# One store of twelve score tiles, a cubic for the exponentials of one attention and one product for both: gated pair of attentions on one core

## The chip, the core and the metric

The kernel runs on one core of a Trainium2 chip. The metric is the device time of one execution in microseconds; the median of three executions before the change is 1826.78 us (1826.64 to 1827.12).

## The reference

Two attentions, A and B, read the same x (2048 tokens of 512 values, 32 heads of 16). A has one key and one value head for all its query heads, B has its own for each. A gate per token mixes them.

```python
def _A_ref(x, wq, wk, wv, wo):
    ...
    scores = jnp.einsum("bhqd,bkd->bhqk", q, k) * (Dh ** -0.5)
    p = _softmax(scores, axis=-1)
    o = jnp.einsum("bhqk,bkd->bhqd", p, v)
    return (lambda x, *d: x.transpose(*d))(o, 0, 2, 1, 3).reshape(B, S, H * Dh) @ wo
...
g = _sigmoid((x * gate_w).sum(-1, keepdims=True))
a = _A_ref(x, A_wq, A_wk, A_wv, A_wo)
b = _B_ref(x, B_wqkv, B_wo)
return g * a + (1 - g) * b
```

All of it is float32. The weights A_wq and A_wk are drawn eight times larger than the others, so the scores of A are large and those of B small.

## The kernel before

**The work.** The heads of each attention go in four groups of eight, in the order A0, B0, A1, B1 and so on. A group goes through four phases (two halves of 1024 queries, each with two sets of four heads); there are 32 phases. A phase has 32 quads, two for each block of 128 keys; a quad is two score tiles of 128 x 1024, so there are 2048 score tiles. For each, TensorE makes the scores (`products`, eight matmuls of 64x32 with 512 columns in float16, into one of two PSUM banks `sc`), then the exponential goes to SBUF. When both tiles of a quad are there, its V product (`values`, float32) adds to a PSUM accumulator `pair[0]`; the ones among the columns of V give the softmax denominators in the same product.

**Two ways to an exponential.** Most tiles go through ScalarE (`score`, one ACTIVATE of 128 x 1024). The others go through VectorE (`chain`): the scores land in the spare bank `pair[1]`, and seven VectorE instructions make the exponential: a conversion to an integer, two bit operations that part exponent and mantissa, and four multiply-adds (`horner`). ScalarE writes into six tiles `prob`, VectorE works in six tiles `vec`.

**Beside it** run the projections of the next group (24 jobs of eight matmuls for each half of q, k and v, `project`), their layout by DMA, and for each finished half of a group the output products (`o_unit`): for each of four pairs of token blocks six jobs of eight matmuls into the spare bank, VectorE multiplies by the gate into one of two tiles `sums`, and a DMA adds that to the output in HBM. Ahead of it `normalised` brings the accumulator's rows in place by DMA, takes reciprocals of 128 x 512 denominators and multiplies. The last output, that of group B3, is added on chip to what HBM held (`late`), and written.

**The order** of each engine's instructions is written out by a planner in the kernel (`_Plan`, `pe_step`, `spare_job`, `value_job`), which goes by costs (`EXP`, `HALF`, `PRODUCT`) and due times. The next score stands at the earliest where a bank comes free; other work may stand ahead of it as long as it starts at most SLACK = 404 ns after the start of the ACTIVATE before it. For the second score of a quad this lateness holds only for V products of VectorE's quads (the lines with `LATE`). A V product stands whole (512 columns) where 860 ns are left up to the next score, else as two halves of 256.

Of the kernel before, what the change touches and what calls it, by code (L numbers as in the profile page):

```python
# [20 lines left out]
P = 128  # L21
# [6 lines left out]
NG = 4  # L28
# [7 lines left out]
S_MAX = 40.0  # L36


VEC = (0.14718679, 0.3602188, 0.76941108, -0.03925424)
LEAD = struct.unpack("I", struct.pack("f", 3.46474126))[0] & 0x7FFFFF  # L40
# [3 lines left out]
EXP, EXP_ENDS, EXP_AFTER = 904, 1136, 456  # L44
# [6 lines left out]
PROBS, VECS = 6, 6  # L51
# [116 lines left out]
def _fast(ctx, tc, x, wq_a, wk_a, wv_a, wo_a, wqkv_b, wo_b, gate_w, out, flag):  # L168
# [23 lines left out]
    sums = [big.tile([P, 2, BLK], F32, name=f"sum{n}") for n in range(2)]  # L192
# [82 lines left out]
    x_tiles = (vec_tiles + sums)[:8]  # L275
# [145 lines left out]

    def project(part, src, gi, half, kind, can, due):
# [17 lines left out]
        def finish(t):  # L440
# [9 lines left out]
            def then(end):  # L450
                free["spare"] = end + FROM_VEC
                plan.vec(lambda: absmax(kind, 2 * gi + half, hilo[0], AX.XY), 1130, 4, end, due=end + 8000)
                if part == "v":
                    turned(gi, half, hilo, end)
                else:
                    put(hilo, end)
# [6 lines left out]
                     lambda now: ready.get(need, math.inf) <= now and free["hilo"] <= now and can(), due, name, lambda now: can())  # L463

    def turned(gi, half, hilo, now):
# [26 lines left out]
        units.append(_Unit(jobs, finish, lambda now: True, lambda: 0, f"turn{gi}{half}"))  # L492
# [3 lines left out]
    def o_unit(n, half, t, qs, first, last):  # L496

        src, gi = groups[n]
        w, i = weights[src, gi, "o"], "ab".index(src)
        steps = [(q, a, b) for q in qs for a, b in PARTS]  # L500
        tt = [8 * half + t, 8 * half + 4 + t]
        mine = late[:, 4 * half + t]
        state = {}

        def job(k):
            q, a, b = steps[k]
            lhs = [o16s[n, half, q][:, a, t * P : (t + 1) * P]] * 2
            rhs = [w[e ^ (q // 2)][:, b] for e in range(2)]
            by_tiles(pair[1], lhs, rhs, k == 0, k == len(steps) - 1)

        def finish(end):
            def take(e):
                g = gate_up[:, i, tt[e] : tt[e] + 1]
                if n + 1 == len(groups):
                    nc.vector.scalar_tensor_tensor(mine[:, e], pair[1][:, e], g, mine[:, e], op0=ALU.mult, op1=ALU.add)  # L515
                    if last:
                        (nc.sync, nc.scalar)[e].dma_start(out[tt[e] * P : (tt[e] + 1) * P, :], mine[:, e])
                    return
                if e == 0:
                    state["sum"] = sums[state["turn"]]  # L520
                nc.vector.tensor_scalar(state["sum"][:, e], pair[1][:, e], g, None, op0=ALU.mult)  # L521

            def then(t):
                free["spare"] = t + FROM_VEC
                if n + 1 == len(groups):
                    return
                dst = out.rearrange("(h e t p) d -> h t p e d", h=2, e=2, p=P)[half, t_]
                if n == 0:
                    done = plan.on_sp([lambda: nc.sync.dma_start(dst, state["sum"])], t, ISSUE_SP)
                else:  # L530
                    done = plan.on_pool([lambda: nc.gpsimd.dma_start(dst, state["sum"], accum_op=ALU.add)], t, 1300)  # L531
                sum_free[state["turn"]] = done + SUM_LANDS

            t_ = t
            begin = end + TO_VEC
            if n + 1 < len(groups):
                state["turn"] = turn[0]
                turn[0] ^= 1
# [6 lines left out]
        due = 32 * (4 * n + 2 * half + 8)  # L545
        return _Unit(jobs, finish, lambda now: all(made(("o16", n, half, q), math.inf) <= now for q in qs)
                     and made(("wo", src, gi), math.inf) <= now and made("gates", math.inf) <= now
                     and (sum_free[turn[0]] <= now + 4000 if n + 1 < len(groups) else made("late", math.inf) <= now), lambda: starts_in(due), f"o{n}{half}{t}")

    turn, sum_free = [0], [0.0, 0.0]  # L550

    def normalised(n, half, q, raw, now):
# [10 lines left out]
        moves = [(*move, e) for t in (d, o) for e in range(2) for move in moves if move[0] is t]  # L563
        for m, (part, at, to, n_rows, e) in enumerate(moves):
            queues[m % len(queues)].dma_start(part[ROWS * e + to :][:n_rows], raw[at, e])
        plan.sp = max(plan.sp, now) + len(moves) * ISSUE_SP
        o16 = ops.tile([P, 2, BLK], F16, tag="o16", name=f"o16{n}{half}{q}", bufs=7)
# [5 lines left out]

        def times(c):
            nc.vector.scalar_tensor_tensor(o[:, c : c + cut], o[:, c : c + cut], UP, d[:, c : c + cut], op0=ALU.mult, op1=ALU.mult)
# [10 lines left out]
        due = now + 30000  # L586

# [3 lines left out]
        for c in range(0, BLK, cut):  # L591
            a = plan.vec(lambda c=c: over(c), 1560, 3.5, now + 7700, (), None, due)
            b = plan.vec(lambda c=c: times(c), 330, 3.4, now + 12000, (a,), None, due)
            e = plan.vec(lambda c=c: high(c), 200, 3.3, 0.0, (b,), None, due)
# [873 lines left out]
```

## Time and profile before

| what | value |
|---|---|
| median of three executions | 1826.78 us |
| span of the profiled execution | 1822.2 us |
| so outside the span, against the median | 4.6 us |
| ScalarE busy | 1778.7 us, 98% |
| TensorE busy | 1742.1 us, 96% |
| VectorE busy | 1332.0 us, 73% |
| score tiles on ScalarE / on VectorE | 1926 / 122 |

The profile gives one time for the profiled execution, its span, from the first to the last instruction. "Busy" of an engine is the time in which at least one of its instructions was under way; a matmul's end is modelled, so TensorE's share says little on how much room it has. A group of rows names its source line, the engine, what was written from what, the shapes, the count, the busy time and the mean time of one. A float32 product appears as two matmuls per matmul of the source. "issue" as a releaser means that nothing in the profile explains the wait.

### The profile page before, as it was taken

What the parts mean: (1) busy time and instruction counts of PE and PEld (TensorE: products, weight loads), DVE (VectorE), ACT (ScalarE), POOL (GpSimd) and SP (SyncE); (2) the same over time, 40 slices, a digit from 0 to 9 for tenths busy, and PEclk for the clock granted to TensorE, in tenths of its full rate; (3) what the DMA queues carried; (4) which work ended last, traced back from release to release, by engine and by line L of the source; (5) the groups of instructions that cost most, each with busy time, mean ns of one, the idle gap of its engine ahead of it and who ended that gap; (6) DMA issues with size and microseconds to landing.
All of it is one profiled execution on the core that took longest, in us unless ns stands there. A gap on an engine that the chain in (4) does not pass through costs nothing.

```text
span 1822.2 us, 95700 instructions
## 1 busy us (share of the span) xinstructions
PE 1742.1 (96%) x44697; PEld 844.5 (46%) x44697; DVE 1332.0 (73%) x1507; ACT 1778.7 (98%) x1942; POOL 305.1 (17%) x367
## 2 busy tenths in 40 slices
PE   8999999999999999999999999999999999999896
PEld 5544444444444444444444444444444444444442
DVE  5277656779667597869767569796967676788994
ACT  5999999999999999999999999999999999999995
POOL 2212001202020131231102023133200111012000
PEclk9999999999999999999999999999999999999998
DMA  5121111323121142433212123342312122236111
GB/s 152 36 61 44 46 58 55 90 55 67 32 62 32 39 83 55 75 65 66 44 42 63 32 66 56 67 84 63 64 20 57 44 55 57 42 67 149 36 61 61
DMA packets 64883, 109.39 MB, mean 60 GB/s; under 512 B 14480, under 2 KB 22928, under 8 KB 64480
## 3 DMA queue, kind: packets, MB, share of 16 engines
q0 software_dynamic: 21504, 43.99, 13.6%
q1 hardware_dynamic: 39744, 56.99, 11.4%
q8 instruction: 351, 5.75, 1.3%
q10 hardware_dynamic: 3232, 2.23, 0.4%
q14 instruction: 52, 0.43, 0.1%
HBM read 14.75 MB, written 33.55 MB: 27 GB/s over the span
## 4 chain that ended last, share of the span: by engine, by line
ACT 86%; issue 8%; PE 4%; DVE 1%; DMA 1%; ACTq 0%; POOL 0%; DVEq 0%
ACT prob L641 85%; PE pair L682 1%; PE sc L627 1%; PE pair L301 0%; DVE vec L856 0%; PE pair L1173 0%; DMA prob<-in_A_wv_dram 0%; DVE xT L1295 0%; DMA vec<-in_A_x_dram 0%; DVE xT L515 0%; DMA Qa<-loqa 0%; PE pair L335 0%; DVE dT L572 0%; ACT early L641 0%; PE pair L210 0%
## 5 line engine op out<-in xcount | busy, mean ns | idle before, releaser
L641 ACT ACTIVATE prob<-sc 128x1024 f32<-128x1024 f32 x1905 | 1749.7, 1134 | 3.8 <-PE sc L627 3.2
L682 PE MATMUL pair<-prob,vA 64*32 64x512 f32 (+1 forms) x8048 | 510.4, 566 | 0.0
L682 PE MATMUL pair<-prob,vB 64*32 64x512 f32 (+1 forms) x8016 | 508.4, 569 | 0.0
L856 DVE SCALAR_TENSOR_TENSOR vec<-vec,vec 128x1024 f32<-128x1024 f32 x366 | 445.9, 1242 | 2.8
L627 PE MATMUL sc<-Qb,K 64*32 64x512 f16 x7632 | 395.9, 380 | 37.2 <-ACT prob L641 26.8
L627 PE MATMUL sc<-Qa,kA 64*32 64x512 f16 x7776 | 401.8, 380 | 21.7 <-ACT prob L641 11.6
L627 PEld LDWEIGHTS <-K 64*32 64x32 f16 x8192 | 201.2, 89 | 414.8 <-issue 375.1
L627 PEld LDWEIGHTS <-kA 64*32 64x32 f16 x8192 | 199.8, 89 | 390.2 <-issue 346.6
L843 DVE TENSOR_SCALAR vec<-pair 128x1024 int32<-128x1024 f32 x122 | 148.4, 1216 | 64.5 <-PE pair L627 64.4
L682 PEld LDWEIGHTS pair<-prob,vA 64*32 64x32 f32 x8048 | 155.3, 105 | 20.0 <-issue 1.4
L682 PEld LDWEIGHTS pair<-prob,vB 64*32 64x32 f32 x8016 | 153.5, 105 | 19.0 <-DVE raw L747 0.7
L856 DVE SCALAR_TENSOR_TENSOR vec<-vec 128x1024 f32<-128x1024 f32 x122 | 151.8, 1247 | 0.6
L531 POOL DMA_DIRECT2D out_dram<-sum x48 | 60.6, 1284 | 387.6 <-DVE sum L521 373.0
L572 DVE RECIPROCAL dT<-dT 128x256 f32<-128x256 f32 (+1 forms) x66 | 111.4, 1694 | 18.9 <-DMA dT<-raw 18.6
L747 DVE COPY raw<-pair 128x1024 f32<-128x1024 f32 x31 | 37.9, 1224 | 95.8 <-PE pair L682 95.2
L847 DVE TENSOR_SCALAR vec<-vec 128x1024 int32<-128x1024 int32 x122 | 84.1, 692 | 2.8 <-PE pair L682 1.3
L851 DVE TENSOR_SCALAR vec<-vec 128x1024 int32<-128x1024 int32 x122 | 84.5, 695 | 0.0
L521 DVE TENSOR_SCALAR sum<-pair,gate_up 128x512 f32<-128x512 f32 x112 | 78.6, 740 | 6.3 <-PE pair L210 6.0
L404 POOL DMA_DIRECT2D Qa<-hiqa x31 | 17.3, 558 | 305.6 <-DVE hiqa L445 284.5
L210 PEld LDWEIGHTS <-o 64*32 64x32 f16 x3072 | 50.1, 93 | 39.3 <-ACT o L578 8.1
L404 POOL DMA_DIRECT2D Qb<-hiqb x32 | 18.4, 574 | 293.3 <-DVE o L578 169.1
L210 PE MATMUL pair<-w16ob,o 64*32 64x512 f16 x1488 | 61.1, 384 | 6.0 <-ACT o L578 6.0
(160 smaller groups left out, 1182.7 us busy)
## 6 DMA issues: line engine op xcount, KB each, us to landing
out_dram<-sum POOLq DMA_DIRECT2D x48, 512.0 KB, 5.8
vB<-vB SPq DMA_DIRECT2D x16, 384.0 KB, 4.9
dT<-raw SPq DMA_DIRECT2D x32, 128.0 KB, 3.1
oT<-raw SPq DMA_DIRECT2D x32, 128.0 KB, 3.4
out_dram<-sum SPq DMA_DIRECT2D x8, 512.0 KB, 2.9
xT<-out_dram SPq DMA_DIRECT2D x16, 256.0 KB, 3.3
dT<-raw SPq DMA_DIRECT2D x62, 64.0 KB, 2.2
out_dram<-xT SPq DMA_DIRECT2D x12, 256.0 KB, 2.4
```

The source lines that it names most:

```text
L210: nc.tensor.matmul(outs[n : n + COLS, i], lhs[i][rows(i), n : n + COLS], rhs[i][rows(i)], start=start, stop=stop)
L521: nc.vector.tensor_scalar(state["sum"][:, e], pair[1][:, e], g, None, op0=ALU.mult)
L531: done = plan.on_pool([lambda: nc.gpsimd.dma_start(dst, state["sum"], accum_op=ALU.add)], t, 1300)
L572: nc.vector.reciprocal(d[:, c : c + cut], d[:, c : c + cut])
L627: nc.tensor.matmul(bank[a : a + COLS, hh], k[rows(hh), key : key + COLS], Q[src, gi, half, p][rows(hh), j * BLK : (j + 1) * BLK], start=Tr ...
L641: nc.scalar.activation(probs[u], sc, AF.Exp, scale=SCALE / (UP * UP))
L682: nc.tensor.matmul(pair[0][32 * k : 32 * k + 32, i, cols], v[rows(i)], probs[2 * m + k // 2][rows(i), hh, cols], start=first, stop=last)
L747: nc.vector.tensor_copy(state["raw"], full)
L843: nc.vector.tensor_scalar(tile("p").bitcast(I32), pair[1], SCALE / (UP * UP) / math.log(2) * 2.0 ** 23, None, op0=ALU.mult)
L847: nc.vector.tensor_scalar(tiles["m"].bitcast(I32), tiles["p"].bitcast(I32), 0x7FFFFF, 125 << 23, op0=ALU.bitwise_and, op1=ALU.bitwise_or)
L851: nc.vector.tensor_scalar(tiles["w"].bitcast(I32), tiles["p"].bitcast(I32), 0x7F800000, 0x40000000 | LEAD, op0=ALU.bitwise_and, op1=ALU.bi ...
L856: nc.vector.scalar_tensor_tensor(p, m if i == 3 else p, VEC[i], m if i else w, op0=ALU.add, op1=ALU.mult)
```

## The change

- **A cubic for B.** The exponential of a VectorE tile of B is a cubic in its score, made by three VectorE instructions; A keeps the seven. The kernel's flag, which sends inputs out of range to a general path, now also asks that for B the largest sum of |q| over a head times the largest |k| stays under `B_MAX / SCALE` = 0.64 (`magnitudes` takes that sum with a small product).
- **One store.** `prob` and `vec` tiles become one pool of twelve, `free_tiles`. ScalarE may write into a tile that VectorE had, and the other way round. A chain holds three tiles (A) or two (B). The rule that kept three `vec` tiles back goes.
- **Gate and denominators.** The denominators go through DRAM (`held`, `back`) into 128 x 32 values, where one reciprocal and one multiplication by the gate serve for a block; they are spread again by eight DMAs (`spread`). With the gate inside, the outputs of A and B of a group are summed in one product: `o_unit` has 12 steps for a pair of groups, and three sums go to HBM in place of seven; the last is added on chip in both. `sums` has one tile.
- **The order.** The lateness rule holds for both scores of a quad; spare-bank work (chains, projections, output products) stands ahead of V products where more than `LEFT` tiles are free; `EXP` is 916 in place of 904. Moves of q and k into place are put off until the phase that frees their tiles (`behind`).

The core of the diff:

```diff
+CUBE = (0.5500864384102879, 0.8808852829622843, -0.986763876, 1.22848465)
-EXP, EXP_ENDS, EXP_AFTER = 904, 1136, 456
+EXP, EXP_ENDS, EXP_AFTER = 916, 1148, 456
-PROBS, VECS = 6, 6
+PROBS, VECS, SUMS = 6, 6, 1
+LEFT, LEFT_END, KEPT = 3, 5, 3
...
-        steps = [(q, a, b) for q in qs for a, b in PARTS]
+        steps = [(n, q, a, b) for n, q in done for a, b in PARTS]
...
-            for e in range(2):
-                plan.vec(lambda e=e: take(e), 660, 1, begin, (), then if e else None)
+            plan.vec(take, 1131, 1, begin, (), then)
...
+            for which, count in heads:
+                nc.sync.dma_start(held.rearrange("(e h) q -> h e q", e=2)[to : to + count], raw[which])
+                to += count
+            nc.sync.dma_start(each, held.rearrange("h (c j) -> (h c) j", c=DH))
...
+        def gated():
+            nc.vector.reciprocal(each, each)
+            nc.vector.scalar_tensor_tensor(each, each, UP, gate_in[:, "ab".index(src), half], op0=ALU.mult, op1=ALU.mult)
...
+                nc.sync.dma_start(back.rearrange("h (c j) -> (h c) j", c=DH), each)
+                for e in range(2):
+                    for h in range(4):
+                        at = h if src == "a" else h % 2 * 2 + h // 2
+                        nc.sync.dma_start(d[ROWS * e + h * DH :][:DH], back[4 * e + at : 4 * e + at + 1].to_broadcast([DH, BLK]))
...
-    free_probs, free_vecs, held = deque(prob_tiles), deque(), [0, 0, 0]
+    free_tiles, owed = deque(prob_tiles), [0]
...
-            (free_vecs if m in vector else free_probs).append(tile)
+            free_tiles.append(tile)
...
-        if held[0] > held[2] - 3 or plan.backlog(2) > 2500:
+        if plan.backlog(2) > 2500:
             return None
         u = pick(now)
-        if u is None:
+        if u is None or spare_tiles() < (3 if source(quads[u // 2][0]) == "a" else 2) + (0 if half_vec else KEPT):
             return None
...
+            def first():
+                nc.vector.tensor_scalar(tile("p"), pair[1], CUBE[0] * SCALE / (UP * UP), CUBE[1], op0=ALU.mult, op1=ALU.add)
+            def second():
+                nc.vector.scalar_tensor_tensor(tile("w"), tiles["p"], CUBE[2], tiles["p"], op0=ALU.add, op1=ALU.mult)
+            def third():
+                p, w = tiles["p"], tiles["w"]
+                nc.vector.scalar_tensor_tensor(p, w, CUBE[3], p, op0=ALU.add, op1=ALU.mult)
...
-        first = (spare, mine, other) if begins and len(free_probs) > 1 else (mine, other, spare) if ending else (mine, spare, other)
+        first = (spare, mine, other) if begins and spare_tiles() > 1 or spare_tiles() > (LEFT_END if ending else LEFT) else (mine, other, spare) if ending else (mine, spare, other)
...
-            if part[0] and get is not mine and plan.scant():
-                to = min(to, t + LATE)
```

What the planner makes of it is told by the built program's order of instructions. It is written without times; a row is an instruction with its line, what it writes and what it reads.

**TensorE, a V product in an A phase** (`sc...` are score banks, `Qa...` queries, `vA` the values, `pair` the accumulator). Before, between the last matmul of one score and the first of the next:

```order
L627 MATMUL sc1695_35364<-Qa311_32772,kA_88 32x512
L682 MATMUL pair1_83<-prob4_101,vA0_89 32x512 x4
L682 MATMUL pair1_83<-prob1_98,vA0_89 32x512 x4
L627 LDWEIGHTS kA_88
L627 MATMUL sc1696_35383<-Qa310_32771,kA_88 32x512
```

And after, in the same phase:

```order
L711 MATMUL sc1713_39295<-Qa311_35583,kA_88 32x512
L766 MATMUL pair0_82<-prob2_99,vA1_90 32x256 x4
L766 MATMUL pair0_82<-prob1_98,vA1_90 32x256 x4
L711 LDWEIGHTS kA_88
L711 MATMUL sc1714_39314<-Qa310_35582,kA_88 32x512
```

The product of a quad now stands here in two pieces of 256 columns, each with its own eight matmuls. Over the program 904 quads were whole and 120 in halves; now 421 are whole and 603 in halves. Scores on ScalarE go from 1926 to 1848, on VectorE from 122 to 200 (60 of A, 140 of B). Projections (744 jobs) and output products (384 jobs) keep their number.

**ScalarE, the ACTIVATEs in the middle of the program** with the semaphores that each waits for. Before:

```order
L641 ACTIVATE prob0_97<-sc1035_21830 128x1024 [waits PE_49,Activation_49]
L641 ACTIVATE prob3_100<-sc1036_21849 128x1024 [waits PE_49]
L641 ACTIVATE prob4_101<-sc1037_21876 128x1024 [waits PE_49,Activation_49]
L641 ACTIVATE prob2_99<-sc1038_21895 128x1024 [waits PE_49]
L641 ACTIVATE prob0_97<-sc1039_21922 128x1024 [waits PE_49,Activation_49]
```

And after:

```order
L725 ACTIVATE vec1_104<-sc1039_23838 128x1024 [waits PE_49]
L725 ACTIVATE vec2_105<-sc1040_23884 128x1024 [waits DVE_49,PE_49]
L725 ACTIVATE prob2_99<-sc1041_23910 128x1024 [waits DVE_49,PE_49]
L725 ACTIVATE prob1_98<-sc1042_23937 128x1024 [waits PE_49,Activation_49]
L725 ACTIVATE vec0_103<-sc1043_23972 128x1024 [waits PE_49]
```

ScalarE now writes into tiles of both names, and some ACTIVATEs wait for VectorE: 200 of them, none before. 961 of the 1848 wait for two semaphores or more; before 958 of 1926.

**VectorE at the end of the program** (`xT` is the output tile on chip, `raw31` the copy of the last accumulator). Before:

```order
L581 TENSOR_TENSOR o16710_40935<-oT710_40923,o16710_40935 128x256
L515 SCALAR_TENSOR_TENSOR xT_84<-pair1_83,gate_up_96,xT_84 128x512 x8
L744 COPY raw31_42005<-pair0_82 128x512
L572 RECIPROCAL dT712_42009<-dT712_42009 128x128
L575 SCALAR_TENSOR_TENSOR oT712_42008<-oT712_42008,dT712_42009 128x128
```

And after:

```order
L653 TENSOR_TENSOR o16710_44440<-oT710_44426,o16710_44440 128x256
L561 SCALAR_TENSOR_TENSOR xT_84<-pair1_83,xT_84 128x1024 x5
L822 COPY raw31_46010<-pair0_82 128x512
L627 RECIPROCAL dT712_46014<-dT712_46014 128x128
L645 SCALAR_TENSOR_TENSOR oT712_46013<-oT712_46013,dT712_46014 128x128
```

The last thing ahead of the copy of the accumulator is in both a pass over an output product; that product has nine jobs now and had three.

More of the change, by code (lines that the diff above doesn't have):

```diff
@@ L455, in then @@
                 else:
[L456 removed]
+                    s = 2 * (2 * gi + (src == "b")) + half
+                    behind(64 * (s - 1) if part == "q" else 256 * gi, lambda t: put(hilo, max(t, end)))
             free["hilo"] = math.inf
@@ L518, in take, with then @@
                     return
[L519 to L525, printed above, removed]
+                state["sum"] = sums[state["turn"]]
+                nc.vector.tensor_scalar(state["sum"], pair[1], UP ** -2, None, op0=ALU.mult)
+            def then(now):
+                free["spare"] = now + FROM_VEC
+                undone[j, half] -= 1
+                if ends:
@@ L550, in _fast @@
-    turn, sum_free = [0], [0.0, 0.0]
+        due = 32 * (8 * j + 2 * half + 8)
+        undone[j, half] = undone.get((j, half), 0) + 1
+        return _Unit(jobs, finish, lambda now: all(made(("o16", n, half, q), math.inf) <= now and made(("wo", *groups[n]), math.inf) <= now for n, q in done)
+                     and (made("late", math.inf) <= now if ends else sum_free[turn[0]] <= now + 6000), lambda: starts_in(due), f"o{j}{half}{t}")
+    undone = {}
+    turn, sum_free = [0], [0.0] * SUMS
     def normalised(n, half, q, raw, now):
@@ L586, in normalised, with spreads @@
         due = now + 30000
+        begun = [math.inf]
         def then(end):
             ready["o16", n, half, q] = end + FROM_VEC
[L591 to L594, printed above, removed]
-            plan.vec(lambda c=c: low(c), 330, 3.2, 0.0, (e,), then if c else None, due)
+        def spreads(end):
+            spread(end)
+            for c in range(0, BLK, cut):
+                b = plan.vec(lambda c=c: times(c), 330, 3.4, begun[0], (), None, due)
+                e = plan.vec(lambda c=c: high(c), 200, 3.3, 0.0, (b,), None, due)
+                plan.vec(lambda c=c: low(c), 330, 3.2, 0.0, (e,), then if c else None, due)
+        plan.vec(gated, 430, 3.5, now + 7500, (), spreads, due,
+                 room=lambda: ready.get("gates", math.inf) <= plan.dve)
     tail = []
```

227 lines of the change are left out of this document (149 added, 78 removed).

## The prediction

> **What bounds the kernel now.** I read the page's first and fourth parts, then the groups of rows, then the timelines of ScalarE and TensorE.
>
> ```profile
> span 1822.2 us, 95700 instructions
> PE 1742.1 (96%) x44697; PEld 844.5 (46%) x44697; DVE 1332.0 (73%) x1507; ACT 1778.7 (98%) x1942; POOL 305.1 (17%) x367
> ACT 86%; issue 8%; PE 4%; DVE 1%; DMA 1%; ACTq 0%; POOL 0%; DVEq 0%
> ```
>
> The chain that ended last is ScalarE's. TensorE's 96% is not full work: its rows follow. In the groups, ScalarE's exponentials hardly wait for anything; TensorE's scores are the ones that wait, for ScalarE:
>
> ```profile
> L641 ACT ACTIVATE prob<-sc 128x1024 f32<-128x1024 f32 x1905 | 1749.7, 1134 | 3.8 <-PE sc L627 3.2
> PE sc L627 <- ACT prob L641: 38.4, 108, 0.5
> ```
>
> ScalarE's own timeline gives the sum: its first exponential, a long unbroken run, its last.
>
> ```profile
> 28.11 5.66 ACT L641 ACTIVATE prob<-sc 128x1024 f32<-128x1024 f32 x6 [1.20 <-PE sc L627]
> 299.37 121.23 ACT L641 ACTIVATE prob<-sc 128x1024 f32<-128x1024 f32 x132
> 1796.94 3.90 ACT L641 ACTIVATE prob<-sc 128x1024 f32<-128x1024 f32 x4
> ```
>
> In the run 132 ACTIVATEs take 121.23 us; less the last one's own 1.13, that is 120.10 / 131 = 0.917 us from start to start. The last exponential ends at 1796.94 + 3.90 = 1800.84, so it starts at 1799.7. So the span is 28.1 of head, 1925 steps x 0.917 = 1765.2, gaps of 1799.7 - 28.1 - 1765.2 = 6.4, and from the last start to the end 22.5. Outside the span lie 1826.8 - 1822.2 = 4.6 us; I add them at the end.
>
> **The change, part by part.**
>
> *ScalarE's share.* 1848 exponentials in place of 1926: 78 x 0.917 = 71.5 us less. 961 of 1848 wait on two semaphores where 958 of 1926 did, half in both, so I keep 0.917.
>
> *VectorE, which takes the 78.*
>
> ```profile
> L843 DVE TENSOR_SCALAR vec<-pair 128x1024 int32<-128x1024 f32 x122 | 148.4, 1216 | 64.5 <-PE pair L627 64.4
> L847 DVE TENSOR_SCALAR vec<-vec 128x1024 int32<-128x1024 int32 x122 | 84.1, 692 | 2.8 <-PE pair L682 1.3
> L851 DVE TENSOR_SCALAR vec<-vec 128x1024 int32<-128x1024 int32 x122 | 84.5, 695 | 0.0
> L856 DVE SCALAR_TENSOR_TENSOR vec<-vec,vec 128x1024 f32<-128x1024 f32 x366 | 445.9, 1242 | 2.8
> L572 DVE RECIPROCAL dT<-dT 128x256 f32<-128x256 f32 (+1 forms) x66 | 111.4, 1694 | 18.9 <-DMA dT<-raw 18.6
> L521 DVE TENSOR_SCALAR sum<-pair,gate_up 128x512 f32<-128x512 f32 x112 | 78.6, 740 | 6.3 <-PE pair L210 6.0
> 1806.04 0.95 DVE L572 RECIPROCAL dT<-dT 128x128 f32<-128x128 f32 x1 [3.20 <-DMA dT<-raw]
> ```
>
> A chain of seven is 1216 + 692 + 695 + 4 x 1242 = 7571 ns, so 122 of them 924 us. The cubic is one read of PSUM and two passes: 1216 + 2 x 1242 = 3700 ns. After: 60 x 7.57 + 140 x 3.70 = 972, 48 more. The big reciprocals go (111.4, less 4 x 0.95 that stay); their 31 small successors I bound above by two passes of the 128x128 one, 31 x 1.9 = 59. The gated sums go from 112 x 0.74 = 83 (79 by busy time) to 24 x 1.24 = 30. Sum: 1332 + 48 - 108 + 59 - 49 = 1282 at most, 73% of 1763. VectorE as a whole does not become the bound.
>
> *TensorE.* Its jobs of eight matmuls, by their starts:
>
> ```profile
> 703.13 0.41 PE L627 MATMUL sc<-Qb,K 64*32 64x512 f16 x8
> 703.34 1.06 PE L210 MATMUL pair<-xT,w16qb 64*32 64x512 f16 x32
> 705.17 1.06 PE L682 MATMUL pair<-prob,vB 64*32 64x256 f32 x32
> 1797.43 1.05 PE L682 MATMUL pair<-prob,vB 64*32 64x512 f32 x16
> ```
>
> The score starts at 703.13, the next job at 703.34: 0.215 us with the rounding, and four projection jobs or four passes of 256 columns take the same 1.06. Two passes of 512 take 1.05, that is 0.428 each. So two halves cost the array what a whole product costs, and the work is 2048 scores, 1024 V products of four units, 744 projection and 384 output jobs: 7272 x 0.215 = 1564 us, the same before and after. Against ScalarE's run it is 89% before, and 1564 / 1693 = 92% after. By phases, counted from the order: at most 91% before, as 226 units (48.6 us) against 58 ACTIVATEs (53.2 us) in the second phase of B0; after, the fullest reach 97%, as 240 units (51.6 us) against 58 ACTIVATEs in the last phase of B0 to B2. No stretch of 64 ACTIVATEs before the last asks for more of the array than ScalarE leaves. But there is less of a cushion: with both scores of a quad allowed as late as ScalarE has work, a stop of TensorE is passed on to ScalarE where before every other score had room. The small new jobs (eight for `magnitudes`, one for the gates) are 2 us of a TensorE that has 100 free.
>
> *What is late next: TensorE's instructions.* Halving the V products doubles their instructions: 1144 pieces become 1627, each of 16 matmuls and 16 weight loads, so 44697 pairs become about 52460. The page has a queue for them, and one stretch in the head shows TensorE starved:
>
> ```profile
> q8 instruction: 351, 5.75, 1.3%
> 46.69 0.37 PE L335 MATMUL pair<-wkv,xT 64*128 64x33 f16 x16 [0.66 <-issue]
> 46.99 0.41 PE L627 MATMUL sc<-Qa,kA 64*32 64x512 f16 x8
> 47.33 0.47 PE L335 MATMUL pair<-wkv,xT 64*128 64x33 f16 x24
> 47.73 0.41 PE L627 MATMUL sc<-Qa,kA 64*32 64x512 f16 x8
> 48.07 0.78 PE L335 MATMUL pair<-wkv,xT 64*128 64x33 f16 x48
> 48.78 0.41 PE L627 MATMUL sc<-Qa,kA 64*32 64x512 f16 x8
> 49.12 0.37 PE L335 MATMUL pair<-wkv,xT 64*128 64x33 f16 x16
> 50.14 0.27 PE L335 MATMUL pair<-wkv,xT 64*128 64x33 f16 x8 [0.65 <-issue]
> ```
>
> 89394 instructions over 351 packets is 255 each. Between the two unexplained stops, both in the middle of a row of like matmuls, lie 16 + 8 + 24 + 8 + 48 + 8 + 16 = 128 matmuls with as many weight loads: 256 instructions in 50.14 - 46.69 = 3.45 us. So a starved TensorE gets 256 / 3.45 = 74 a microsecond. A packet took on the mean 0.013 x 16 x 1822 / 351 = 1.08 us; where DMA is busy it takes longer, and the rate falls. What is asked:
>
> ```profile
> 300.00:600.00 300.00, 290.75 (x7528) 140.40 (x7514) 224.36 (x243) 299.84 (x328) 45.00 (x53) 1.00 0.24 58
> ```
>
> Before, 15042 / 300 = 50 a microsecond. After, phases ask 47 to 72 (the first phase of A3: 3744 instructions in 60 x 0.917 = 55.0 us, 68). I cut the new order into blocks of 64 ACTIVATEs and took for each block what its instructions need beyond 64 x 0.917. Summed: 0 us at a supply of 72 or more, 4 at 68, 12 at 66, 26 at 64, 54 at 62, 89 at 60, 131 at 58. I take 68, a little under the starved rate since packets lengthen, so 4 us; the range keeps 0 and 54.
>
> [...]
>
> *The shared store.* 200 ACTIVATEs wait for VectorE where none did. Behind such an ACTIVATE stand all of ScalarE's, and the next score waits for its bank. A wait costs nothing if VectorE keeps the planner's order, up to a pass of 1.24 us if it is one behind: 0 to 248 us. The nearest row is ScalarE's waits for TensorE, 3.2 us over 1905. I take 25 ns each, 5 us. VectorE itself now waits at `take` for the one `sum` tile's landing; its chains and the copies of the accumulator queue behind that. 24 such waits of at most one pass are 30 us on an engine that is idle for a quarter, so nothing here.
>
> *DMA queues.* SP issues about 297 more DMAs (248 spreads of denominators among them).
>
> ```profile
> 703.94 1.10 SPq L565 DMA_DIRECT2D dT<-raw  x2
> L531 POOL DMA_DIRECT2D out_dram<-sum x48 | 60.6, 1284 | 387.6 <-DVE sum L521 373.0
> ```
>
> At 0.55 us each that is 163 us of SP. Behind a block's 13 to 18 of them (up to 10 us) stand half of the moves of q and k; those are made a phase of 50 us ahead, which hides it. Without that cover the start of a half group would wait 10 us, 15 times. The gates' 33 DMAs (18 us of SP) come once, under the first phases; only the first output products wait for them, a group later. POOL loses 32 issues of 1.28 us that nobody waited for.
>
> *The end.*
>
> ```profile
> 1799.05 0.41 PE L627 MATMUL sc<-Qb,K 64*32 64x512 f16 x8
> 1802.16 0.68 DVE L744 COPY raw<-pair 128x512 f32<-128x512 f32 x1
> ```
>
> The copy of the last accumulator came 3.1 us after the last score began. In the order 10 units of 0.215 stood between them; now it is 27 (13 of them output products), 5.8 us, and a pass over the last of these, 1.24 us after about 5.4, comes before the copy: it starts at 6.6, so 3.5 later.
>
> *The sum.* 28.1 + 1847 x 0.917 (1693.7) + 6.4 + 22.5 + 3.5 + 4 + 5 = 1763.2 us of span, and with 4.6 outside it **1767.8 us**.
>
> **The rivals.**
>
> *The supply never limits.* As a mechanism of this kernel, blocks land before they are wanted, since even at full array work TensorE takes 16 instructions per 0.215 us, the 74 that the starved stretch got. For it: at 50 a microsecond no stop outside the head; against it: the two stops. It gives 1767.8 - 4 = 1764; with a free store, 1759. [...]
>
> *The supply is 62 to 64.* For it: the 74 of the head was measured without the new spreads, whose packets share the DMA engines; against it: a block would have to take 4.0 to 4.1 us in place of 3.45. It gives 26 to 54 in place of 4: 1790 to 1818.
>
> *The store couples the engines.* If the 200 waits cost 0.15 to 0.25 us, ScalarE gains gaps of 30 to 50 us: 1793 to 1813. For it: VectorE waits for TensorE now and then (64 us at L843); against it: a quarter of VectorE is idle, so it catches up.
>
> *Slower.* Supply under 61 a microsecond, a block in 4.2 us in place of 3.45, through DMA traffic that meets each packet: the gain of 71.5 - 3.5 - 5 is then eaten. At 58 it gives 1763.8 + 131 = 1895. A packet's mean would have to be 1.08 + 0.7 us or more; the mean of the profile's page speaks against it.
>
> *The change falls to the general path.* From the reference's inputs, B's largest sum of |q| over a head is 1.49 and its largest |k| 0.271: 0.40 against 0.64. So it does not; a time for it has no row here.
>
> **How the numbers follow.** Forecast 0.45; supply never limits 0.2; supply of 62 to 64 0.16; coupled store 0.13; slower 0.04; general path 0.01; another gain lost in the head 0.01. The range holds the first two with the store's waits free (1759, less up to 6 if the gaps of the head close: 1753) and most of the next two: 1753 to 1805. A measurement of this kernel tells 0.2%, 3.7 us, from no change; only a supply close to 61 would come so near. Faster 0.94, same 0.02, slower 0.04.
>
> **What would show it.** Right: ScalarE's ACTIVATEs 0.917 us apart in long runs, 1848 of them; the last score 6 to 7 us ahead of the copy of the accumulator; the instruction queue with about 410 packets; few waits of ScalarE for VectorE. Wrong: rows of TensorE with "issue" ahead of them in the middle of like matmuls in the A phases, above all where 68 or more a microsecond are asked; ScalarE idle behind VectorE's passes for more than 20 us; a phase start where scores wait for a DMA into Q.

## The result and the profile after

The changed kernel takes 1792.66 us (median of four executions, 1790.59 to 1794.08), the kernel before 1826.74 on the same chip: a ratio of 0.982, 95% interval 0.9808 to 0.9831. The forecast was 1767.8, so 24.9 us of the expected gain did not come. The profiled execution has a span of 1790.1 us, 26.9 more than the 1763.2 of the sum.

The profile's page of the changed kernel: span, engines, the instruction queue, the chain by engine, and ScalarE's two groups.

```profile
span 1790.1 us, 111592 instructions
PE 1710.0 (96%) x52459; PEld 1020.9 (57%) x52459; DVE 1257.3 (70%) x1409; ACT 1717.2 (96%) x1864; POOL 259.9 (15%) x335
q8 instruction: 412, 6.75, 1.6%
PE 38%; ACT 35%; DVE 13%; issue 10%; DMA 2%; SPq 1%; DVEq 0%; ACTq 0%; POOL 0%; POOLq 0%
L725 ACT ACTIVATE prob<-sc 128x1024 f32<-128x1024 f32 x939 | 947.4, 1096 | 17.7 <-PE sc L711 14.4
L725 ACT ACTIVATE vec<-sc 128x1024 f32<-128x1024 f32 x898 | 911.5, 1096 | 12.7 <-PE sc L711 10.3
```

The chain was ScalarE's for 86% and is now TensorE's and ScalarE's in turn. ScalarE waits 14.4 + 10.3 = 24.7 us for scores where it waited 3.2. What holds the scores up is seen on TensorE's timeline (above) and ScalarE's (below) at the same place:

```profile
1274.17 0.84 PE L215 MATMUL pair<-w16oa,o 64*32 64x512 f16 x24
1274.82 0.41 PE L711 MATMUL sc<-Qb,K 64*32 64x512 f16 x7
1276.41 0.39 PE L711 MATMUL sc<-Qb,K 64*32 64x512 f16 x1 [1.18 <-issue]
1276.42 0.81 PE L766 MATMUL pair<-prob,vB 64*32 64x256 f32 x16
```

```profile
1274.43 1.15 ACT L725 ACTIVATE vec<-sc 128x1024 f32<-128x1024 f32 x1
1276.84 1.02 ACT L725 ACTIVATE vec<-sc 128x1024 f32<-128x1024 f32 x1 [1.25 <-PE sc L711]
```

Seven of a score's eight matmuls run, the eighth comes 1.18 us later, and nothing in the profile explains it: all eight read from the same two tiles, and the eighth waits for no semaphore. ScalarE stands 1.25 us. Numbered from TensorE's first instruction, these unexplained stops all come at one and the same place of a block of 256 instructions, as do those in the head of the kernel before. From the last start ahead of a stop to the first behind it, 34 of them are over 0.3 us and make 24.7 us; the kernel before has 10 with 5.1 us. What TensorE asks for, from the windows view (the columns are busy time and instructions of PE and PEld, then DVE, ACT, POOL):

```profile
300.00:600.00 300.00, 293.96 (x9363) 180.30 (x9353) 190.99 (x209) 296.61 (x323) 30.45 (x39) 1.00 0.19 50
```

(9363 + 9353) / 300 = 62 instructions a microsecond, where the kernel before asked 50. The instruction queue's 412 packets stand against TensorE's 2 x 52459 instructions, 255 a packet, about the length of that block; a stop at that place is called a fetch below.

I took all of ScalarE's gaps apart in the trace: each ACTIVATE that starts over 20 ns later than 0.917 us after the one before it, by the holes that TensorE had ahead of its score. A hole at the 256th instruction counts as fetch; one at an instruction that waits for a semaphore (mostly a spare bank that VectorE frees) as semaphore; no hole at all counts as a full array; "ScalarE" is a gap that begins after the score was there. "All" is the sum of all steps less 0.917 each; it is lower than the sum of the parts, because many steps are a little under 0.917 us (11 us in all in the changed kernel). Which part a gap falls to hangs on which hole is set beside it: with a slightly different rule the fetch part is 24 in place of 27.0 after and 36 in place of 43.6 in the first experiment, so single entries are good to some us.

| kernel | packets | scores | fetch | semaphore | array full | ScalarE | other | all |
|---|---|---|---|---|---|---|---|---|
| before | 351 | 1926 | 1.7 | 1.4 | 2.0 | 2.8 | 2.4 | 6.7 |
| after | 412 | 1848 | 27.0 | 10.6 | 5.6 | 7.4 | 2.3 | 41.7 |

Theory 1: the missing time is TensorE's supply of instructions. Rival 1: it is the engines waiting for each other over the tiles of the store and the spare bank. Rival 2: the rate is enough, and a fetch hurts only where it comes late behind a large transfer.

### The profile page after: what moved, and what is told of

Its sections match the earlier page's. It is cut to its first block, busy times and chain, and to the rows that moved or that the text cites. A ratio compares the mean times of both kernels' runs of the same rounds, so it can differ in the third digit from the quotient of the medians.

```text
span 1790.1 us, 111592 instructions
## 1 busy us (share of the span) xinstructions
PE 1710.0 (96%) x52459; PEld 1020.9 (57%) x52459; DVE 1257.3 (70%) x1409; ACT 1717.2 (96%) x1864; POOL 259.9 (15%) x335
## 4 chain that ended last, share of the span: by engine, by line
PE 38%; ACT 35%; DVE 13%; issue 10%; DMA 2%; SPq 1%; DVEq 0%; ACTq 0%; POOL 0%; POOLq 0%
PE pair L766 19%; ACT prob L725 18%; ACT vec L725 17%; PE sc L711 10%; PE pair L215 8%; DVE vec L956 2%; DVE vec L936 2%; DVE prob L956 1%; DVE prob L959 1%; DVE vec L959 1%; DVE vec L963 1%; DVE prob L936 1%; DVE prob L963 1%; SPq L639 1%; PE pair L711 1%
## 5 line engine op out<-in xcount | busy, mean ns | idle before, releaser
L725 ACT ACTIVATE prob<-sc 128x1024 f32<-128x1024 f32 x939 | 947.4, 1096 | 17.7 <-PE sc L711 14.4
L725 ACT ACTIVATE vec<-sc 128x1024 f32<-128x1024 f32 x898 | 911.5, 1096 | 12.7 <-PE sc L711 10.3
L766 PE MATMUL pair<-prob,vA 64*32 64x256 f32 (+1 forms) x6680 | 458.2, 422 | 2.1 <-issue 1.4
L766 PE MATMUL pair<-vec,vA 64*32 64x256 f32 (+1 forms) x6688 | 454.5, 421 | 1.8 <-issue 1.6
L766 PE MATMUL pair<-prob,vB 64*32 64x256 f32 (+1 forms) x6344 | 445.7, 445 | 0.1
L766 PE MATMUL pair<-vec,vB 64*32 64x256 f32 (+1 forms) x6168 | 429.8, 439 | 0.5 <-issue 0.3
L766 PEld LDWEIGHTS pair<-vec,vA 64*32 64x32 f32 x6688 | 187.1, 106 | 31.3 <-issue 3.9
L766 PEld LDWEIGHTS pair<-vec,vB 64*32 64x32 f32 x6168 | 164.5, 106 | 27.7 <-issue 2.9
L956 DVE TENSOR_SCALAR vec<-pair 128x1024 f32<-128x1024 f32 x78 | 94.9, 1217 | 15.7 <-PE pair L711 12.2
L215 PE MATMUL pair<-xT,w16kb 64*32 64x512 f16 x1536 | 81.7, 376 | 0.5 <-issue 0.5
```

The source lines that it names most:

```text
L215: nc.tensor.matmul(outs[n : n + COLS, i], lhs[i][rows(i), n : n + COLS], rhs[i][rows(i)], start=start, stop=stop)
L725: nc.scalar.activation(probs[u], sc, AF.Exp, scale=SCALE / (UP * UP))
L766: nc.tensor.matmul(pair[0][32 * k : 32 * k + 32, i, cols], v[rows(i)], probs[2 * m + k // 2][rows(i), hh, cols], start=first, stop=last)
L956: nc.vector.tensor_scalar(tile("p"), pair[1], CUBE[0] * SCALE / (UP * UP), CUBE[1], op0=ALU.mult, op1=ALU.add)
```

## The experiments

All ratios are to the kernel before, on the same chip, with 95% intervals.

**V products always in halves, in the kernel before.**

```diff
-        wide = BLK if n == 0 and plan.scant() and room + TIGHT - SLACK >= 2 * HALF else BLK // 2
+        wide = BLK // 2
```

> The kernel before, with every V product in two halves of 256 columns in place of 904 whole ones. Array work, scores on ScalarE (1926) and semaphores stay; TensorE's instructions go from about 89400 to about 118000, 66 a microsecond. Theory 1 (the supply of instructions to TensorE is what the change ran into): about 460 instruction packets and 20 to 60 us more than the kernel before, 1847 to 1887 us, with stops of TensorE in the middle of like matmuls every 256 instructions. Rival 1 (the missing time is engines waiting for each other over tiles and the spare bank): 1827 us, within 4 us, since none of that is touched. Rival 2 (a fetch hurts only when it is late behind a large transfer, the rate itself is enough): under 10 us more.

Measured: 1864.15 us against 1824.86, ratio 1.0218 (1.02 to 1.0236). 464 packets. Halving, without the store, the cubic or the new order, and more of it than the change has (1024 quads in halves against 603), costs 39 us, so it is dear by itself. Rival 2's figure (under 10 us) falls, and so does rival 1 for what halving costs. TensorE's timeline of this run has two stops in a row, each behind the first matmul of a score:

```profile
829.71 0.38 PE L627 MATMUL sc<-Qb,K 64*32 64x512 f16 x1
830.41 0.41 PE L627 MATMUL sc<-Qb,K 64*32 64x512 f16 x7 [0.32 <-issue]
830.43 0.81 PE L682 MATMUL pair<-prob,vB 64*32 64x256 f32 x16
830.88 0.57 PE L627 MATMUL sc<-Qb,K 64*32 64x512 f16 x8
831.10 1.23 PE L682 MATMUL pair<-prob,vB 64*32 64x256 f32 x32
831.96 0.58 PE L627 MATMUL sc<-Qb,K 64*32 64x512 f16 x8
832.18 0.80 PE L682 MATMUL pair<-prob,vB 64*32 64x256 f32 x16
832.86 0.41 PE L627 MATMUL sc<-Qb,K 64*32 64x512 f16 x8
833.08 1.06 PE L682 MATMUL pair<-prob,vB 64*32 64x256 f32 x32
833.94 0.38 PE L627 MATMUL sc<-Qb,K 64*32 64x512 f16 x1
834.70 0.41 PE L627 MATMUL sc<-Qb,K 64*32 64x512 f16 x7 [0.39 <-issue]
```

From the first stop's end to the second's are 7 + 16 + 8 + 32 + 8 + 16 + 8 + 32 + 1 = 128 matmuls, with their weight loads 256 instructions, in 834.70 - 830.41 = 4.29 us: 60 a microsecond, not the 74 that the prediction read from the head.

**Whole products may come later (560 ns in place of 404).**

```diff
-SLACK, TIGHT, URGENT = 404, 404, 300
+SLACK, TIGHT, URGENT = 404, 560, 300
```

> The changed kernel, where a whole V product of ScalarE's quads may hold the next score back to 560 ns after an ACTIVATE's start in place of 404: 770 quads whole in place of 421, about 11000 instructions fewer, 1850 scores on ScalarE in place of 1848. Theory 1: the stops go where the demand falls under the supply; 15 to 30 us less than the changed kernel, 1763 to 1779 us, about 370 instruction packets, although some scores come up to 100 ns later. Rival 1: 1794 us plus up to 20 for the later scores, since tiles and the spare bank are used as before. Rival 2: the number of late fetches falls with the packets, by a tenth: 1789 to 1793 us.

Measured: 1796.95 us, ratio 0.9843 (0.9825 to 0.986), no gain, as rival 1 had it. The table below shows why: the gaps behind fetches fell from 27.0 to 12.5 us, but the array was late for 15.6 in place of 5.6, and semaphores took 15.4 in place of 10.6. The prediction of theory 1 for the time failed, since the edit is not free; its prediction for the stops held.

**And whole products ahead of the spare bank's work.**

```diff
+        whole = mine() if not begins else None
+        first = (mine, spare, other) if whole and whole[1] > HALF else (spare, mine, other) if begins and spare_tiles() > 1 or spare_tiles() > (LEFT_END if ending else LEFT) else (mine, other, spare) if ending else (mine, spare, other)
```

> As the run with 560 ns, and a whole V product that fits stands ahead of the spare bank's work: 856 quads whole, 14000 instructions fewer than the changed kernel, 1838 scores on ScalarE (9 us less by the count). Theory 1: 25 to 38 us less than the changed kernel, 1755 to 1768 us. Rival 1: 1783 us by the count of scores, and more if the spare bank's work comes later. Rival 2: 1780 to 1783 us.

Measured: 1787.91 us, ratio 0.9797 (0.978 to 0.9813). The fetch gaps fell to 6.9, the others rose to 47. Theory 1's time is missed by 20 us and rival 2's by 5; the time fits rival 1 (1783 and more), the fetch gaps fit theory 1.

**The lateness rule back, in the changed kernel.**

```diff
+            if part[0] and get is not mine and plan.scant():
+                to = min(to, t + LATE)
```

> The changed kernel with the old rule that a second score of a quad is not held back: 1896 scores on ScalarE in place of 1848 (44 us more by the count), 441 quads whole, instructions nearly the same (107300 against 108000 by the order). Theory 1: TensorE has the cushion again, so part of the gaps of ScalarE (41.7 us beyond the pitch of 0.917) goes: 1812 to 1830 us. Rival 1: the waits for VectorE's passes over the spare bank stay: 1834 to 1838 us.

Measured: 1822.59 us, ratio 0.9991 (0.998 to 1.0001). The time is as theory 1 had it. With nearly as many instructions (410 packets) the fetch gaps halve to 14.2 and the semaphores' fall to 1.7, against rival 1. But TensorE's own stops halve too (those over 0.3 us from 34 with 24.7 us to 16 with 12.2), so this run does not show that a cushion hides a fetch. The kernel before does: its 5.1 us of such stops cost ScalarE 1.7. The 48 scores that ScalarE keeps in this run cost more than the gaps that went. So nearly all of the change's gain hangs on this one step.

**Transfers in pieces.**

```diff
-                done = plan.on_sp([lambda: swapped(vB[1][:, ts], vB[0][:, ts], nc.sync)], end, 2 * ISSUE_SP)
+                done = plan.on_sp([lambda k=k: swapped(vB[1][:, 8 * half + 2 * k :][:, :2], vB[0][:, 8 * half + 2 * k :][:, :2], nc.sync) for k in range(4)], end, 2 * ISSUE_SP)
...
-                    at = plan.on_pool([lambda: nc.gpsimd.dma_start(dst, state["sum"], accum_op=ALU.add)], now, 1300)
+                    at = plan.on_pool([lambda e=e, r=r: nc.gpsimd.dma_start(dst[rows(r), e], state["sum"][rows(r), e], accum_op=ALU.add) for e in range(2) for r in range(2)], now, 325)
```

> The changed kernel with its large transfers in pieces: the swap of a half of V for B (2 DMAs of 384 KB) as 8 of 96 KB, each sum for HBM (512 KB) as 4 of 128 KB. Bytes, the order of all engines' work and the 1848 scores stay. Theory 1 in its sharper form (a fetch of 256 instructions hurts most when it stands behind a transfer that fills the 16 DMA engines; of 18.9 us in TensorE's stops of over 0.45 us, 16.0 came with the engines half full or more): 1782 to 1788 us, with 4 or fewer stops of TensorE over 1 us. If the rate alone limits, whatever else the DMA engines do: 1791 to 1795 us, as the changed kernel. If the many more issues on SP and POOL come late for someone: 1796 us or more.

Measured: 1793.63 us, ratio 0.9829 (0.9817 to 0.9842), as the changed kernel. From the last start ahead of a stop to the first behind it, the stops over 1 us did go, from seven to two (the longest from 1.96 to 1.07), but smaller ones came in their place: those over 0.45 us went from 20 with 19.4 us to 24 with 15.8, and the fetch gaps only from 27.0 to 25.1. The sharper form of theory 1 falls by its time: at this rate of instructions most of the loss stays without the large transfers. Besides, ScalarE stands 2.49 us here:

```profile
1721.91 1.14 ACT L725 ACTIVATE vec<-sc 128x1024 f32<-128x1024 f32 x1
1725.14 0.36 ACTq L564 DMA_DIRECT2D out_dram<-xT  x1
1725.55 1.94 ACT L725 ACTIVATE vec<-sc 128x1024 f32<-128x1024 f32 x2 [2.49 <-DMA dT<-back]
```

The ACTIVATE does not read the denominators `dT`. What stands is ScalarE's own issue of an output DMA (L564, the row above it), by the profile until a copy of the denominators has landed. The changed kernel does not stand there, but the control below, whose transfers are whole, does (2.3 us), and so do both runs with 560 ns above (2.1 and 2.9); so the pieces need not be the cause.

**Whole products first, up to 460 ns** (the third run's line, and 460 for 560).

> The changed kernel, where a whole V product that fits stands ahead of the spare bank's work and may hold the next score back to 460 ns after an ACTIVATE's start (with 456 ns from a score's start to its ACTIVATE that is the pitch of 0.917): 594 quads whole in place of 421, 5500 instructions fewer, 1856 scores on ScalarE (7 us more by the count). Theory 1: half of the 27 us of ScalarE's gaps behind fetches goes and nothing comes for it, as it did at 560 ns: 1784 to 1790 us. Rival 1 (tiles and the spare bank): 1798 to 1802 us by the count of scores.

Measured: 1794.37 us, ratio 0.9826 (0.9812 to 0.9841), between the two. The fetch gaps fell to 10.4 and the array is on time (4.8), but ScalarE's own waits rose to 14.2, and 8 more scores cost 7.

**A wider margin for VectorE.**

```diff
-TO_VEC, FROM_VEC, CHAINED = 255, 150, 130
+TO_VEC, FROM_VEC, CHAINED = 255, 400, 130
```

> The changed kernel, where the planner takes 400 ns in place of 150 from a VectorE instruction's end to the use of what it freed: 1858 scores on ScalarE (9 us more by the count), instructions as before (107600 against 108000 by the order). Rival 1 in what is left of it (TensorE waits for the spare bank that VectorE frees, 10.6 us of ScalarE's gaps): that term falls to 3 us, so 1792 to 1796 us. If the waits don't come from this margin: 1800 to 1803 us. Theory 1 says nothing of it but that the gaps behind fetches stay at 20 to 27 us.

Measured: 1809.46 us, ratio 0.9909 (0.9893 to 0.9924), slower than either expectation. The semaphores' part fell to 7.8 only, the fetch gaps stayed (28.4), and ScalarE's own waits doubled to 14.6. A wider margin does not take the waits for the spare bank away; why the run is 6 us slower even than the count of scores has it stays open.

**Pieces and whole products up to 460 ns together.**

> The two edits together: transfers in pieces, and whole V products ahead of the spare bank's work up to 460 ns. 1856 scores on ScalarE. Theory 1: the gaps behind fetches fall from 27 to under 8 us: 1776 to 1784 us, faster than both kernels. Rival 1: 1798 to 1802 us.

Measured: 1787.5 us, ratio 0.9797 (0.978 to 0.9814); the fetch gaps are 7.4, all gaps 28.1. Theory 1's time (1776 to 1784) is missed by 4 us, rival 1's by more. Here the pieces seem to help: 7 us against the run without them, at the edge of the two intervals.

**Half the instructions for the same order.** A halved V product from 8 matmuls in place of 16.

```diff
+                    t, lhs, to = high_half(t).unsqueeze(1).to_broadcast([ROWS, 2, BLK // 2]), high_half(lhs), slice(0, BLK)
+                    row = 32 * (k // 2) + (64 if cols.start else 0)
```

> The changed kernel, same order of all engines, with each of the 1206 halved V products made of 8 bfloat16 matmuls of 512 columns in place of 16 float32 ones of 256. Two of the eight follow each other on each of four tile positions, so that the array should be taken as long as before (0.43 us), with half the instructions (16 in place of 32). It leaves out the low halves of V and of the exponentials and sums a head's rows in another place, so that its output is not the reference's; only its time counts. TensorE's pairs fall from 52459 to about 42800, under the 44697 of the kernel before; the scores (1848), the transfers, the tiles and VectorE's work stay. Theory 1 (instruction supply): about 336 packets, gaps of ScalarE behind fetches from 27 us to under 4, 1762 to 1774 us. Rival 1 (tiles, the spare bank, late scores through a full array): 1789 to 1797 us, as the changed kernel.

Measured: 1769.59 us, ratio 0.9702 (0.9688 to 0.9715): 23 us less than the changed kernel and within 2 us of the 1767.8 that were forecast for the change. Page and window:

```profile
PE 1679.0 (95%) x42811; PEld 826.4 (47%) x42811; DVE 1257.6 (71%) x1409; ACT 1710.0 (97%) x1864; POOL 261.4 (15%) x335
q8 instruction: 337, 5.52, 1.4%
300.00:600.00 300.00, 291.59 (x7680) 145.71 (x7675) 190.47 (x210) 298.12 (x326) 32.43 (x47) 1.00 0.19 52
```

51 instructions a microsecond. The fetch gaps are 2.1 us, while semaphores (11.0) and ScalarE's own waits (7.7) are those of the changed kernel. Where a halved product stands alone ahead of a score, it is 0.62 us in the median from its first matmul to the score's (0.55 in the changed kernel, 0.68 in the control below). So against the changed kernel the array did not become freer, and the time does not follow this figure.

**Its control: the same data and positions, 16 matmuls again.**

```diff
+                for part_of in to:
+                    nc.tensor.matmul(pair[0][row : row + 32, i, part_of], lhs, t, start=begin and part_of.start == 0, stop=end and part_of.stop == BLK)
```

> The control of the run with half the instructions: the same bfloat16 data, the same four tile positions and the same columns in all, but each of its 8 matmuls of 512 columns as two of 256, so that a halved V product has 32 instructions again (52459 pairs in all, about 412 packets). It leaves out the same part of the computation. Only the number of instructions differs from that run. Theory 1: the gaps of ScalarE behind fetches come back, 20 to 35 us, 1787 to 1803 us. If the gain of that run came from a freer array or from the 16-bit data: 1769 to 1774 us.

Measured: 1792.58 us, ratio 0.9822 (0.9804 to 0.984), the changed kernel's time to 0.1 us.

```profile
PE 1700.2 (95%) x52459; PEld 1063.7 (59%) x52459; DVE 1256.8 (70%) x1409; ACT 1717.1 (96%) x1864; POOL 254.9 (14%) x335
q8 instruction: 412, 6.75, 1.6%
300.00:600.00 300.00, 291.54 (x9320) 185.43 (x9312) 189.18 (x208) 295.18 (x321) 29.62 (x39) 1.00 0.19 50
```

By their code the two runs differ only in how many matmuls make a halved product; the fetch gaps are back with 23.2 us, 21.1 more, and all other parts stay within 2 us. With that the cause of 1792.6 - 1769.6 = 23 us (22 by the two ratios) is shown: the number of TensorE's instructions.

**Two candidates: pieces, and whole products first up to 560 and 520 ns.**

> Candidate for a version faster than both: transfers in pieces, whole V products ahead of the spare bank's work up to 560 ns; 1838 scores on ScalarE, 859 quads whole. Theory 1: the gaps behind fetches go to under 5 us, the late scores that the run with 560 ns showed (about 18 us) stay: 1776 to 1784 us. Rival 1: as the run with 560 ns and no pieces, 1786 to 1790 us.

> The same at 520 ns: 1844 scores on ScalarE, 707 quads whole. Theory 1: gaps behind fetches under 8 us, late scores about 10 us: 1776 to 1784 us. Rival 1: 1788 to 1792 us.

Measured: 560 ns 1778.35 us, ratio 0.9739 (0.9725 to 0.9753), faster than both kernels (the changed one's interval begins at 0.9808); 520 ns 1792.01 us, ratio 0.9826 (0.9813 to 0.984), where rival 1 had it and not theory 1, though the fetch gaps went as theory 1 said (4.0). At 560 ns the instruction queue has nearly the packets of the kernel before:

```profile
q8 instruction: 357, 5.85, 1.4%
300.00:600.00 300.00, 289.68 (x7948) 152.09 (x7955) 222.95 (x241) 296.91 (x322) 36.68 (x39) 1.00 0.19 47
```

(7948 + 7955) / 300 = 53 a microsecond, and fetch gaps of 0.1 us. It pays with late scores. The 520 ns run loses to ScalarE's waits (20.2); why just there was not tried.

The run with 560 ns differs from the third run by the pieces alone, at as many packets (357 and 358): 1778.35 against 1787.91 us, with intervals that do not meet, fetch gaps of 0.1 against 6.9, and TensorE's stops over 0.3 us 2 with 1.1 us against 9 with 8.5. So large transfers are part of the cause and not only of the place: with fewer instructions the pieces take away what is left of the stops, while at the changed kernel's 412 packets they won no time. To this extent rival 2 holds.

The gaps of all runs in us, as above:

| run | packets | scores | fetch | semaphore | array full | ScalarE | other | all |
|---|---|---|---|---|---|---|---|---|
| halves in before | 464 | 1926 | 43.6 | 2.3 | 2.7 | 2.3 | 1.3 | 45.5 |
| 560 ns | 368 | 1850 | 12.5 | 15.4 | 15.6 | 8.5 | 3.7 | 46.3 |
| whole first, 560 | 358 | 1838 | 6.9 | 12.9 | 18.8 | 13.7 | 2.0 | 43.8 |
| lateness rule back | 410 | 1896 | 14.2 | 1.7 | 1.1 | 8.5 | 2.7 | 21.7 |
| pieces | 412 | 1848 | 25.1 | 8.8 | 5.3 | 10.2 | 3.2 | 43.6 |
| whole first, 460 | 390 | 1856 | 10.4 | 7.3 | 4.8 | 14.2 | 9.4 | 37.6 |
| margin 400 | 410 | 1858 | 28.4 | 7.8 | 7.8 | 14.6 | 2.6 | 53.0 |
| pieces, whole 460 | 390 | 1856 | 7.4 | 8.5 | 5.7 | 8.5 | 9.7 | 28.1 |
| half the instructions | 337 | 1848 | 2.1 | 11.0 | 3.7 | 7.7 | 5.6 | 19.0 |
| control | 412 | 1848 | 23.2 | 9.9 | 4.0 | 9.0 | 6.1 | 40.1 |
| pieces, whole 560 | 357 | 1838 | 0.1 | 14.7 | 16.1 | 14.6 | 3.0 | 39.4 |
| pieces, whole 520 | 376 | 1844 | 4.0 | 11.0 | 12.4 | 20.2 | 8.2 | 44.0 |

## Why the prediction was right and wrong

**ScalarE's share** was right: 1848 scores at 0.917, 71.5 us less. **VectorE** too: 1257 us busy against at most 1282.

**TensorE's instructions** is the step that failed, in its size: 4 us taken, 22 to 23 by the two runs that differ in nothing else (27.0 in the gaps). The mechanism, the number of packets (412 against about 410) and the stops in the middle of like matmuls were as the prediction had them. Where they come in the program was half right: of the stops over 0.3 us two thirds lie in A's groups (15.7 of 24.7 us), but group A3, where most is asked (63 a microsecond), has only 1.8 us. The time falls into the range of the rival "the supply is 62 to 64" (1790 to 1818), and into the forecast's own range only because that was made wide enough for this rival.

What made the term too small is read from the packets of the instruction queue, set beside the blocks in order. In the changed kernel a block lasts TensorE 4.02 us in the median, in the kernel before 5.06. The next block's packet begins 0.92 us after the block does (median) and takes 1.04 us. At the 20 stops of over 0.45 us it took no longer, 0.97 us, but began 2.3 us after, and in that time other packets kept the 16 DMA engines 84% busy (medians). The kernel before has as many packets that began over 1.5 us after the block ahead, 48 against 50; but only 2 stops of over 0.45 us stand behind them there, and 16 in the changed kernel. So a late packet is nothing new: the shorter block exposes it. A mean over 64 ACTIVATEs, 59 us, in which 14 blocks go by, does not show a single late packet. The 74 a microsecond were read where the DMA engines were nearly idle (6% busy, by the windows view of 46.69 to 50.14 us); in the run with halves two stops lay a block at 60 apart. And the guard against it, a packet's mean time, could not see this, because the packet waits to begin and hardly grows: 0.016 x 16 x 1790 / 412 = 1.11 us after and 1.08 before. Beside busy engines a packet does take longer, as the prediction has it, but by little: in the kernel before 1.08 us on the mean where other packets kept the 16 engines under 5% busy meanwhile, and 1.23 us where over 75% (248 and 23 packets); after, 1.08 and 1.22 us (246 and 13). That the other transfers make packets late is read from when they come, and borne out by the two runs that differ by the pieces alone.

Where 50 and 51 instructions a microsecond are asked (300 to 600 us), the fetch gaps of the whole run are 1.7 us (the kernel before) and 2.1 us (half the instructions); where 62 are asked, 27.0 us (the changed kernel). So the rival "the supply never limits" does not hold at 62.

**The shared store** was put at 5 us of ScalarE behind VectorE, and at nothing for TensorE. The waits view after:

```profile
ACT vec L725 <- DVE vec L963: 1.2, 2, 0.6
ACT prob L725 <- DVE prob L963: 0.7, 1, 0.7
ACT prob L725 <- DVE vec L963: 0.6, 1, 0.6
ACT prob L725 <- DVE prob L936: 0.4, 1, 0.4
ACT prob L725 <- DVE vec L936: 0.4, 1, 0.4
DVE oT L647 <- DMA dT<-back: 23.0, 7, 8.7
```

ScalarE waits 1.2 + 0.7 + 0.6 + 0.4 + 0.4 = 3.3 us for VectorE, so the 5 us were about right. But TensorE, for which nothing was taken, waits at semaphores for 10.6 us of ScalarE's gaps, where it was 1.4. Half the instructions left these 11 us standing, so they are a second, smaller cost. Where they come from was not shown: VectorE's wait for the spread denominators, 23.0 us, is little more than the 18.6 us that it waited for denominators before (L572 in the prediction's rows).

**The end** was right to 0.1 in the step that was worked out and 1.6 short in all. The last score and VectorE's way to the copy:

```profile
1761.89 0.42 PE L711 MATMUL sc<-Qb,K 64*32 64x512 f16 x8
1767.47 1.22 DVE L561 SCALAR_TENSOR_TENSOR xT<-pair,xT 128x1024 f32<-128x1024 f32 x1 [2.57 <-PE pair L215]
1768.61 0.68 DVE L822 COPY raw<-pair 128x512 f32<-128x512 f32 x1
```

The copy starts 1768.61 - 1761.89 = 6.7 us after the score (predicted 6.6), behind the pass over the output product as said. From the last ACTIVATE's start to the end are 27.6 us; 22.5 + 3.5 = 26.0 were forecast.

**The sum**, mended: 27.4 of head, 1693.3, gaps of 41.7 and an end of 27.6 are 1790. Forecast were 28.1, 1693.7, 15.4 (6.4 + 4 + 5) and 26.0. Nearly all of the difference, 26.3, is in the gaps.

## What to carry to other kernels

Here splitting a matmul cost the array nothing (the prediction's rows: 1.06 us for four passes of 256 columns, 1.05 for two of 512) and the instruction stream a whole second set. Before trading wide pieces for fitting ones, compare how long a block of 256 instructions lasts with how late its packet can come (here 4.02 us, and 2.3 us at the stops), not only with how long a packet takes on the mean (1.1 us). The kernel before had 5.1 us of stops over 0.3 us and fetch gaps of 1.7 us, the changed kernel 24.7 and 27.0: when a change takes away the slack between two engines, price the stops of before, not only the new work. A counterfactual with the same order and fewer instructions, with its control, settles in two runs what reading the trace leaves open.

## What the runs showed of the hardware

- A starved TensorE got a block of 256 instructions in 3.45 us in the head, where the DMA engines were 6% busy, and in 4.29 us in the stretch shown of the run with halves, though a packet itself takes 1.1 us on the mean (1.08 in the kernel before, 1.11 in the changed one).
- Over the whole span (two instructions for each of TensorE's pairs): at 48 to 51 a microsecond the stops cost ScalarE 0.1 to 6.9 us (half the instructions, the kernel before, whole first at 560 ns with pieces and without); at 52 to 57, 4.0 to 14.2; at 58 to 59, 23.2 to 28.4 (the changed kernel, pieces, the control, the margin); at 64, 43.6 (halves in the kernel before).
- The stops of over 0.45 us in the changed kernel came where an instruction packet began late (16 of 20 behind one that began over 1.5 us after the block ahead; 2.3 us in the median, against 0.92 over all packets) while other transfers held the DMA engines (84%, median); the packet itself took no longer (0.97 us against 1.04, medians). Smaller transfers cut TensorE's stops over 0.3 us in all three pairs of runs (24.7 to 19.5 in the changed kernel, 15.4 to 5.7 with whole products first up to 460 ns, 8.5 to 1.1 up to 560 ns); in time they won 0, 7 and 10 us.
